# A gated feed-forward kernel: three w1 subtractions moved from a chunk's end to its first steps, and one w2 sum rounded a step sooner

## The chip, the cores and the metric

The kernel runs on one core of a Trainium2 chip. A core has TensorE (matmuls, called PE in the profile; its weight loads are PEld), VectorE (DVE), ScalarE (ACT), GpSimd (POOL) and SyncE (SP), which issues most of the transfers. Each engine works through its own list of instructions in order and waits on semaphores; an instruction that waits holds up all that stand behind it on its engine. The metric is device time in microseconds (us) of one execution, lower is better. A profiled execution leaves a trace in which every instruction has a start and a duration.

## The reference

x has 2048 rows of 576 numbers. The rows are normalised (xn), and two branches work on xn: a linear attention with 32 heads, and a feed-forward network with a hidden width of 4608. The feed-forward part is the one in which the change acts.

```python
xn = _layernorm(x, axis=-1)
s = _A_ref(xn, A_wqkv, A_wo)                      # linear attention, then @ wo
h = _gelu(einsum("bsd,df->bsf", xn, w1) + b1)     # 576 -> 4608
g = _silu(einsum("bsf,fd->bsd", h, w2) + b2)      # 4608 -> 576
return x + s * g
```

## The kernel before

**Products.** Every fp32 operand is split into a high part (a cast to the format that TensorE reads, `set_hi` on ScalarE, L921) and a low part (the rest, `set_lo` on VectorE, L924), and a product is made of three matmuls: high x high, high x low, low x high. Besides, each product of 2 x 2 blocks is made with seven block products in place of eight (a Strassen scheme), so sums and differences of blocks of x, w1, w2 and of the hidden tiles are needed as operands. The products are numbered 1 to 7.

**Stages.** The first 280 us or so are the attention branch. Then the feed-forward network runs over two halves of the 2048 rows, and in each half over nine chunks of 512 hidden columns (`step` counts the 18 chunks; `half, c = divmod(step, 9)`). A chunk has two column pairs for the first product (class `Up`, L1147): each pair needs seven operands from w1. Then come the seven block products with w2 (function `product`, matmuls at L1287, tiles `pm`), in the order 1, 2, 7, 4, 5, 3, 6, each twice (for two groups of rows). VectorE adds each result to `macc` (L1295 or L1297; in chunk 0 L1302 to L1306). Products 2, 3 and 4 go on in the PSUM banks of products 1, 5 and 7: product 3 adds to what product 5 left, and so must wait until VectorE has read product 5's result out of the bank.

**Weights, first half only.** In the first half the chunks also prepare the operands from w1 and w2 for the chunk that follows; they are stored to DRAM too, and the second half only loads them. For w1, a pair n is an object of class `W1`: its raw block (640 KB, tile `w1raw`, L932) is loaded by SyncE into one of two buffers; `T(i)` makes four differences on GpSimd (5 at L946 into the tile `w1t5`, 6 at L948 into `w1t6`, 7 at L951 in place, 4 at L954 in place); `hi(i)` and `lo(i)` round the operands a, 6, 7, 5, b and 4, and `lo` stores each. `w1t5` and `w1t6` exist once each, so a pair's difference 5 waits until the difference 5 of the pair before has been split. The difference 4 overwrites raw data that the operand a reads, and so must follow `lo("a")`. A chunk works on two pairs: in its first steps on its own second pair (table `P1`), and later on the first pair of the next chunk (table `P0`). For w2, `load_sum`, `sum4` and `sum7` build two sums by transfers that accumulate (L497, issued on GpSimd; `sum4(1)` adds the second sum to the first, with which the operand 4 is whole), and `hi` and `lo` round the operands.

**Hidden tiles.** Class `HOps` makes the sums of the hidden tiles on GpSimd: `S(7)` at L1254, `S(5)` at L1245, `S(6)` at L1248, `S(3)` at L1251, for each pair; they wait for the gelu on ScalarE (L1155), and `hi` and `lo` round them (tiles `h_h`, `h_l`).

**What sets the order.** A chunk has 28 steps (`NS`): steps 0 to 6 follow the seven products of the first pair, 7 to 13 those of the second, and 14 to 27 the fourteen of w2. A list `plans` holds what is to be issued behind each step (`add(step, fn)`, `at_step(step)`), in the order of the adds. Order is kept as written on VectorE, ScalarE, GpSimd and TensorE by `in_order`; SyncE's transfers follow the order in which they were issued. So the tables of numbers are the order of the program. `plan_w1` puts a pair's T, hi and lo at the steps of its table, and is itself called at a step, since the pair's object has to exist by then.

Of the kernel before, what the change touches and what calls it, by code (L numbers as in the profile page):

```python
# [42 lines left out]
def linear_attention_gated_ffn(ctx, tc, x, wqkv, wo, w1, b1, w2, b2, out):  # L43
# [97 lines left out]
    class Weight:  # L141
# [28 lines left out]
        def sums(self, raw, eng):  # L170
# [6 lines left out]
            a, b = self.t  # L177
            T = {4: a[:, 0], 5: a[:, 1], 6: b[:, 0], 7: b[:, 1]}
            for i, u, v in ((5, f1a, f0a), (6, f1b, T[5]), (7, f1b, f1a), (4, f0b, T[6])):
                eng.tensor_tensor(T[i], u, v, op=SUB)  # L180

# [339 lines left out]
    def add(step, fn, *args):  # L521
        plans.setdefault(step, []).append((fn, args))

    def at_step(step):
        for fn, args in plans.pop(step, ()):
            fn(*args)
# [191 lines left out]
    for p in range(1, NPAIR):  # L718
        plan_pair(p)
        base = p * NSP  # L720
# [36 lines left out]
    base = NPAIR * NSP  # L757
# [100 lines left out]
    def transpose_p(r, s):  # L858
        pb = p_bufs[s]
        pt = psT.tile([P, 1024], F32, tag="pt", name=f"ptp{r}{s}")  # L860
        for k in range(KT):
            nc.tensor.transpose(pt[:, k * P : (k + 1) * P], pb[:, k * P : (k + 1) * P], ident)
        th = t2.tile([P, KT, P], F32R, tag="th", name=f"th{r}{s}", bufs=3)
        tl = t2.tile([P, KT - 1, P], F32R, tag="tl", name=f"tl{r}{s}", bufs=3)
        pT[r, s] = (th, tl)
        pts[r, s] = pt[:, : KT * P].rearrange("p (k c) -> p k c", k=KT)
# [59 lines left out]
    class W1:  # L926
# [10 lines left out]

        def T(self, i):

            a, b = slice(0, 2), slice(2, 4)  # L940
            f0, f1, src = self.f0, self.f1, self.src
            tt = EW1.tensor_tensor
            if i in (5, 6):
                src[i] = w1p.tile([P, 2, P], F32, tag=f"w1t{i}", name=f"w1t{i}", bufs=1)
            if i == 5:
                tt(src[5], f1[:, a], f0[:, a], op=SUB)  # L946
            elif i == 6:
                tt(src[6], f1[:, b], src[5], op=SUB)  # L948
            elif i == 7:
                src[7] = f1[:, a]  # L950
                tt(src[7], f1[:, b], f1[:, a], op=SUB)  # L951
            else:
                src[4] = f0[:, b]
                tt(src[4], f0[:, b], src[6], op=SUB)  # L954
# [39 lines left out]
    w1t, w2_raw0 = {}, []  # L994
# [5 lines left out]
    for r in range(NPAIR + 2):  # L1000
        base = (NPAIR + r) * NSP
# [35 lines left out]
        if 3 <= r <= 7:  # L1037
            n = 2 * r + 3
# [40 lines left out]
        elif r == NPAIR:  # L1079
# [10 lines left out]
            for j in (5, 6, 7):  # L1090
                w.T(j)
            transpose_p(r - 1, 0)
            p_hi(r - 1, 0), p_lo(r - 1, 0)
            pad(1)
            w.hi("a"), w.lo("a")
            w.T(4)
            at.part(7, 14)
# [90 lines left out]
    class W2:  # L1188
# [34 lines left out]
        def load(self, i):  # L1223
            t, self.ops[i] = op_tile(fr, [2, HD], f"w2_{i}", 1, f"w2_{self.n}_")
            nc.sync.dma_start(t.bitcast(F32), w2_dram[self.n % NC, i])
# [215 lines left out]
    def plan_w1(add, w, base, T, hi, lo):  # L1441
        for table, what in ((T, w.T), (hi, w.hi), (lo, w.lo)):
            for i, at in table.items():
                add(base + at, what, i)

    P1 = dict(
        T={5: 0, 6: 0, 7: 1, 4: 2},
# [1 line left out]
        lo={"a": 0, 6: 1, 7: 2, 5: 3, "b": 4, 4: 4},  # L1449
    )  # L1450
    P0 = dict(
        T={5: 24, 6: 24, 7: 25, 4: 25},
        hi={"a": 24, 6: 25, 7: 26, 5: 26, "b": 27, 4: 27},
        lo={"a": 24, 6: 25, 7: 26, 5: 26, "b": 27, 4: 27},
    )
# [18 lines left out]
    def make(cls, table, n):  # L1474
        table[n] = cls(n)
# [7 lines left out]
    for step in range(n_chunks):  # L1483
        half, c = divmod(step, NC)
        base = step * NS
        plain = step == n_chunks - 1
        h = HOps(c)
        if half == 0:
            plan_w1(add, w1t[2 * step + 1], base, **P1)
            w2c = w2t[step]  # L1490
            if not step:
                w2c.src[7] = w2c.B(0, 1)
                add(base + 2, w2c.sum7)
            for i, at in (PW2 if step else PW2_FIRST).items():
                add(base + at, w2c.hi, i)
                add(base + at, w2c.lo, i)
            if step == 0:
                for i, at in W2_SUMS_FIRST.items():
                    add(at, w2t[0].load, i)
        if half == 0 and c < NC - 1:  # L1500
            add(base + 0, make, W1, w1t, 2 * step + 2)
            add(base + 4, make, W1, w1t, 2 * step + 3)
            add(base + 13, lambda n=2 * step + 2: plan_w1(add, w1t[n], base, **P0))
            make(W2, w2t, step + 1)
            nxt = w2t[step + 1]
            add(base + 0, nxt.load_sum, 4)
            add(base + 12, nxt.sum4, 0)
            add(base + 5, nxt.load_sum, 7)
            add(base + 16, nxt.sum7)
            add(base + (8 if step else 10), nxt.load_raw)  # L1510
            add(base + 21, nxt.hi, 2)
            add(base + 21, nxt.lo, 2)
            add(base + 21, nxt.sum4, 1)
            add(base + 27, nxt.hi, 4)
            add(base + 27, nxt.lo, 4)
            for i, at in W2_SUMS_NEXT.items():
                add(base + at, lambda i=i, n=step + 1: w2t[n].load(i))
        elif not plain:
            add(base + (14 if half == 0 else 7), make, W1Loaded, w1t, 2 * step + 2)
            swap = half == 0  # L1520
            add(base + (22 if swap else 14), make, W1Loaded, w1t, 2 * step + 3)
            if step + 2 < n_chunks:
                make(W2, w2t, step + 1)
                for i, at in W2_NEXT.items():
                    add(base + at + 11 * swap, lambda i=i, n=step + 1: w2t[n].load(i))
            else:
                make(W2, w2t, step + 1)
                add(base + 7, w2t[step + 1].load_raw)
        if not plain:
            if half == 0 and c == NC - 1:  # L1530
                for k, at in ((2, 12), (3, 12), (1, 13), (0, 13)):
                    add(base + at, x_swap, k)
                add(base + 25, silu_first, C11)
                for k in range(2):
                    add(base + 26 + k, combine, C12, nc.vector, slice(2 * k, 2 * k + 2))
                    add(base + 26 + k, combine, C21, nc.gpsimd, slice(2 * k, 2 * k + 2))
            for what in ("S", "hi", "lo"):
                for (i, pr), at in PH[what].items():
                    add(base + at, getattr(h, what), i, pr)
        else:  # L1540
            for f in range(CF):
                w2t[step].plain(f)
                add(base + (1, 2, 3, 8)[f], w2t[step].hi, ("p", f))
                add(base + (2, 3, 8, 9)[f], w2t[step].lo, ("p", f))
        if half == 1 and c == 0:
            add(base, silu_first, C12)
            add(base, silu_first, C21)
            add(base, combine, C22, nc.vector, slice(0, 2))
            add(base + 1, combine, C22, nc.vector, slice(2, 4))
            add(base + 1, silu_first, C22)  # L1550
        if half == 1 and 1 <= c <= 8:
            for k in range(2):
                tiles = {}
                def load(k=k, t=7 + c, tiles=tiles):
                    tiles[0] = finish_tiles(k)
                    finish_load(t, k, tiles[0])
                add(base, load)
                add(base + 4, lambda k=k, t=7 + c, tiles=tiles: finish(t, k, tiles[0]))
        if plain:
            for m in (C12, C21, C22):  # L1560
                add(base + 4, combine, m, nc.gpsimd)
            for t, at in enumerate((5, 5, 7, 13, 5, 12, 12, 12)):
                add(base + at, load_xs, t)
            for b, f, at, lo in (
                (0, 0, 7, 8), (0, 1, 8, 9), (1, 0, 10, 10), (1, 1, 10, 11), (0, 2, 11, 12),
                (0, 3, 12, 13), (1, 3, 13, 13), (1, 2, 13, 13),
            ):
                add(base + at, tail_split, b, f)
                add(base + lo, tail_lo, b, f)
        for j in range(CF // 2):  # L1570
            n = 2 * step + j
            u = Up(n, w1t.pop(n), xs)
            for k, i in enumerate(UP):
                u.step(i)
                h.add(j, u.g)
                at_step(base + 7 * j + k)
        if plain:
            break
        held = {}
        for k, i in enumerate(ORDER):  # L1580
            for q2 in (0, 2):
                product(c, i, q2, [h.ops[i, 0], h.ops[i, 1]], w2t[step].ops[i], held)
                at_step(base + 14 + 2 * k + q2 // 2)
# [36 lines left out]
```

## Time and profile before

| what | value |
|---|---|
| median of 3 runs | 1117.99 us (1117.21 to 1118.75) |
| profiled execution, its own time | 1118.17 us |
| span of its trace (first to last instruction) | 1116.4 us |
| TensorE busy | 98% of the span |
| VectorE, ScalarE, GpSimd busy | 73%, 45%, 42% of the span |
| granted TensorE clock | 1.00 |
| HBM read and written | 165.94 MB and 100.01 MB, 238 GB/s over the span |

The profiled execution lies 0.18 us above the median. Its span is 1.8 us shorter than its time; that is start and end around the instructions, which the trace doesn't show. Timeline rows give start, duration, engine, line, operation, what is written and read by the program's names, the shape, the number of instructions, and in brackets the idle time of the engine before it with what ended it. The list of waits gives total, number and longest. The rows of a source line give the least, median and greatest duration in ns, then the first and last start. Chunks are counted from 0; chunk 2 is the one from about 377 to 423 us.

### The profile page before, as it was taken

The page shows a single profiled execution, that of the slowest core. Times are in us where ns is not written, and L with a number is a line of the kernel's source. Part 1 is how long each engine was busy: PE and PEld are TensorE (multiplying, and loading weights), DVE is VectorE, ACT ScalarE, POOL GpSimd, SP SyncE. Part 2 cuts the span into 40 slices and gives each one's busy share as a digit, 9 for nine tenths or more (in the row PEclk, how much of TensorE's full clock was granted, in tenths as well). Part 3 has the DMA queues.
Part 4 walks back from the last instruction along what each step waited for, and adds up shares of the span by engine and source line. Part 5 has one row for each costly group of instructions (what it writes and reads, how often), then busy time and mean ns, then how long its engine had stood idle before and what let it go on. Part 6 is the DMA issues. An engine that isn't in the chain of part 4 may idle for free.

```text
span 1116.4 us, 18757 instructions
## 1 busy us (share of the span) xinstructions
PE 1095.4 (98%) x6924; PEld 1014.2 (91%) x6924; DVE 812.6 (73%) x1242; ACT 504.2 (45%) x913; POOL 466.1 (42%) x419
## 2 busy tenths in 40 slices
PE   8999999999999999999999999999999999999997
PEld 7899999999898898988989889899898998988987
DVE  6877667877688888888888887666475574664766
ACT  6766555554544444454443544424233243242351
POOL 5854433655354353543535433323224133242340
PEclk9999999999999999999999999999999999999999
DMA  5888747785988879588796869978766666766243
GB/s 203 301 261 280 253 135 224 250 285 188 358 270 308 265 236 355 177 296 272 229 357 185 288 235 382 359 252 282 225 204 213 214 200 216 226 200 218 85 142 114
DMA packets 95531, 271.92 MB, mean 244 GB/s; under 512 B 10381, under 2 KB 21133, under 8 KB 93391
## 3 DMA queue, kind: packets, MB, share of 16 engines
q1 hardware_dynamic: 90543, 260.68, 66.2%
q0 software_dynamic: 4896, 10.03, 5.3%
q8 instruction: 55, 0.90, 0.3%
q14 instruction: 37, 0.30, 0.1%
HBM read 165.94 MB, written 100.01 MB: 238 GB/s over the span
## 4 chain that ended last, share of the span: by engine, by line
PE 88%; DVE 4%; DMA 3%; ACT 2%; issue 1%; POOL 1%; SPq 0%; DVEq 0%; POOLq 0%; ACTq 0%
PE pm L1287 30%; PE e L1147 12%; PE a L1147 10%; PE zy L1147 10%; PE pl L411 5%; PE ps_s L894 5%; PE b L1147 4%; PE e L356 2%; DMA xH<-x_dram 2%; PE a L356 2%; PE z L356 2%; PE pd L1410 2%; PE ps_kva L464 1%; PE b L356 1%; DVE h_l L924 1%
## 5 line engine op out<-in xcount | busy, mean ns | idle before, releaser
L921 ACT CAST h_h<-g 128x512 fp32r<-128x512 f32 x204 | 120.1, 621 | 138.9 <-PE pm L1287 137.8
L924 DVE TENSOR_TENSOR h_l<-g,h_h 128x512 fp32r<-128x512 f32 x204 | 159.5, 782 | 0.0
L1295 DVE TENSOR_TENSOR macc<-macc,pm 128x576 f32<-128x576 f32 x128 | 96.2, 751 | 37.7 <-PE pm L1287 36.0
L1254 POOL TENSOR_TENSOR mid<-g 128x512 f32<-128x512 f32 x34 | 43.9, 1292 | 181.6 <-ACT g L1155 181.6
L1147 PE MATMUL a<-xH,wa 128*128 128x512 f32 x360 | 117.2, 390 | 0.5 <-DMA xH<-x_dram 0.5
L1297 DVE TENSOR_TENSOR macc<-pm,macc 128x576 f32<-128x576 f32 x90 | 68.2, 757 | 25.4 <-PE pm L1287 24.4
L1155 ACT ACTIVATE g<-b,b1c 128x512 f32<-128x512 f32 x36 | 24.8, 688 | 125.0 <-DVE b L1173 125.0
L1147 PEld LDWEIGHTS a<-xH,wa 128*128 128x128 f32 x360 | 67.6, 188 | 14.4 <-DMA xH<-x_dram 0.7
L1147 PE MATMUL e<-xSH,wb 128*128 128x512 f32 x216 | 66.6, 390 | 0.2 <-DVE b L1173 0.2
L1164 ACT COPY mid<-a 128x512 f32<-128x512 f32 x36 | 21.2, 588 | 91.2 <-PE a L1147 91.1
L1248 POOL TENSOR_TENSOR g<-g 128x512 f32<-128x512 f32 x34 | 49.5, 1456 | 22.2 <-DVE h_l L924 20.9
L1381 POOL TENSOR_TENSOR fin1l<-fin1h,fin1l 128x288 f32<-128x288 f32 x8 | 6.4, 805 | 121.9 <-DMA fin1l<-s_dram 63.0
L1147 PE MATMUL a<-xL,wa 128*128 128x512 f32 x144 | 56.2, 390 | 0.0
L1251 POOL TENSOR_TENSOR g<-g 128x512 f32<-128x512 f32 x34 | 49.9, 1467 | 13.1 <-DVE h_l L924 11.8
L1167 DVE TENSOR_TENSOR mid<-b,mid 128x512 f32<-128x512 f32 x36 | 24.6, 685 | 37.5 <-PE b L1147 37.4
L1147 PE MATMUL b<-xSH,w 128*128 128x512 f32 x144 | 50.2, 389 | 0.0
L1147 PE MATMUL zy<-xSH,w 128*128 128x512 f32 x144 | 50.2, 389 | 0.0
L1147 PE MATMUL e<-xSH,w 128*128 128x512 f32 x144 | 50.2, 389 | 0.0
L1147 PE MATMUL zy<-xH,w 128*128 128x512 f32 x144 | 50.2, 389 | 0.0
L1147 PEld LDWEIGHTS e<-xSH,wb 128*128 128x128 f32 x216 | 40.5, 188 | 9.0 <-DVE b L1173 0.6
L1245 POOL TENSOR_TENSOR g<-g 128x512 f32<-128x512 f32 x34 | 47.1, 1386 | 2.7
L1155 ACT ACTIVATE g<-e,b1c 128x512 f32<-128x512 f32 x36 | 24.8, 688 | 49.2 <-DVE e L1180 49.2
(932 smaller groups left out, 3594.2 us busy)
## 6 DMA issues: line engine op xcount, KB each, us to landing
op<-w SPq DMA_DIRECT2D x72, 256.0 KB
w<-op SPq DMA_DIRECT2D x72, 256.0 KB
w1raw<-w SPq DMA_DIRECT2D x18, 640.0 KB
w2raw<-w SPq DMA_DIRECT2D x10, 1152.0 KB
op_a<-wa SPq DMA_DIRECT2D x18, 640.0 KB
wa<-op_a SPq DMA_DIRECT2D x18, 640.0 KB
op<-w2o SPq DMA_DIRECT2D x19, 576.0 KB
w2r<-w SPq DMA_DIRECT2D x6, 1152.0 KB
```

Source lines behind the costliest of these rows:

```text
L356: nc.tensor.matmul(ps, st, mv, start=first and n == 0, stop=n == len(seq) - 1, skip_group_check=True,)
L411: nc.tensor.matmul(self.ps[n], st, self.wk(hl, k, n), start=(i == 0), stop=(i == n_all - 1))
L894: nc.tensor.matmul(self.ps[h], st[:, k, :], w[:, k, h * HD : (h + 1) * HD], start=(i == 0), stop=(i == len(self.seq) - 1),)
L921: nc.scalar.copy(pair[0], src)
L924: eng.tensor_tensor(pair[1], src, pair[0].bitcast(F32), op=SUB)
L1147: nc.tensor.matmul(ps.rearrange("p (c j) -> p c j", c=4), st, mv, start=first and n == 0, stop=n == len(seq) - 1, skip_group_check=True,)
L1155: nc.scalar.activation(g, ps, AF.Gelu_apprx_tanh, bias=b1c[:, f : f + 1])
L1248: tt(src[6, pr], src[5, pr], A(0, 0), op=ADD)
L1251: tt(src[3, pr], src[6, pr], A(0, 1), op=SUB)
L1287: nc.tensor.matmul(ps[:, q, :HD], hs[p][st][:, cs], m[:, p, :], start=(n == 0 and i not in CHAIN), stop=(n == len(seq) - 1), skip_group_ch ...
L1295: nc.vector.tensor_tensor(dst, dst, src, op=SUB)
L1297: nc.vector.tensor_tensor(dst, src, dst, op=ADD)
```

## The change

Two entries move, both in the first eight chunks of the first half. The differences 5, 6 and 7 of the next chunk's first w1 pair are issued at steps 5, 5 and 6 and no longer at 24, 24 and 25; for this `plan_w1` is called at step 4, where the second pair's raw load is issued also. The difference 4 and all roundings of that pair stay at steps 24 to 27. And the operand 4 of the next chunk's w2 is rounded at step 26 and no longer at 27.

```diff
@@ -1449,7 +1449,7 @@
     P0 = dict(
-        T={5: 24, 6: 24, 7: 25, 4: 25},
+        T={5: 5, 6: 5, 7: 6, 4: 25},
         hi={"a": 24, 6: 25, 7: 26, 5: 26, "b": 27, 4: 27},
         lo={"a": 24, 6: 25, 7: 26, 5: 26, "b": 27, 4: 27},
@@ -1500,7 +1500,7 @@
-            add(base + 13, lambda n=2 * step + 2: plan_w1(add, w1t[n], base, **P0))
+            add(base + 4, lambda n=2 * step + 2: plan_w1(add, w1t[n], base, **P0))
@@ -1511,8 +1511,8 @@
-            add(base + 27, nxt.hi, 4)
-            add(base + 27, nxt.lo, 4)
+            add(base + 26, nxt.hi, 4)
+            add(base + 26, nxt.lo, 4)
```

On GpSimd, from the end of chunk 1 to the beginning of chunk 2 (w1raw_4101 is the raw block of pair 4, w1raw_4177 that of pair 5, w1raw_4605 that of pair 6; L1254 is the first sum of the hidden tiles):

```order
-L946 TENSOR_TENSOR w1t_4501<-w1raw_4101 128x256
-L948 TENSOR_TENSOR w1t_4503<-w1raw_4101,w1t_4501 128x256
-L951 TENSOR_TENSOR w1raw_4101<-w1raw_4101 128x256
-L954 TENSOR_TENSOR w1raw_4101<-w1raw_4101,w1t_4503 128x256
+L954 TENSOR_TENSOR w1raw_4101<-w1raw_4101,w1t_4194 128x256
 L946 TENSOR_TENSOR w1t_4596<-w1raw_4177 128x256
 L948 TENSOR_TENSOR w1t_4598<-w1raw_4177,w1t_4596 128x256
 L951 TENSOR_TENSOR w1raw_4177<-w1raw_4177 128x256
 L954 TENSOR_TENSOR w1raw_4177<-w1raw_4177,w1t_4598 128x256
+L946 TENSOR_TENSOR w1t_4696<-w1raw_4605 128x256
+L948 TENSOR_TENSOR w1t_4698<-w1raw_4605,w1t_4696 128x256
+L951 TENSOR_TENSOR w1raw_4605<-w1raw_4605 128x256
 L1254 TENSOR_TENSOR mid<-g 128x512
```

Pair 4's three differences are gone from the end of chunk 1 (they stand at that chunk's beginning now), its difference 4 stays, and pair 6's three stand in chunk 2 behind those of pair 5 and ahead of the hidden tiles' sums.

On VectorE, the last rows of chunk 1 (w_2__4568 before and w_2__4544 after are the w2 operand 4; w_4 and wb are operands of pair 4; the rows of L1295 read the two results of product 6):

```order
-L924 TENSOR_TENSOR w_4_4544<-w1raw_4101,w_4_4544 128x256
-L924 TENSOR_TENSOR w_4_4546<-w1t_4501,w_4_4546 128x256
-L1295 TENSOR_TENSOR macc<-macc,pm_4554 128x2x288
-L924 TENSOR_TENSOR w_2__4568<-w2s_2_4103,w_2__4568 128x576
+L924 TENSOR_TENSOR w_2__4544<-w2s_2_4103,w_2__4544 128x576
+L924 TENSOR_TENSOR w_4_4549<-w1raw_4101,w_4_4549 128x256
+L924 TENSOR_TENSOR w_4_4551<-w1t_4192,w_4_4551 128x256
+L1295 TENSOR_TENSOR macc<-macc,pm_4559 128x2x288
 L924 TENSOR_TENSOR wb_4575<-w1raw_4101,wb_4575 128x384
```

The subtraction of the w2 operand moved from behind the last read of product 6 to ahead of two w1 parts and of that read. ScalarE's casts move in the same way, and on SyncE the store of the w2 operand goes ahead of the stores of operands 7 and 5 of w1 and of one load.

## The prediction

> **What bounds the kernel now.** I read the page first, then the list of waits, then the matmul groups of the second product, then one chunk's end in the timeline, and last the stretch into which work is moved.
>
> ```profile
> PE 1095.4 (98%) x6924; PEld 1014.2 (91%) x6924; DVE 812.6 (73%) x1242; ACT 504.2 (45%) x913; POOL 466.1 (42%) x419
> ...
> PE pm L1287 <- DVE macc L1295: 6.4, 7, 1.1
> ...
> PE pm L1287 <- ACT h_h L921: 0.7, 1, 0.7
> ```
>
> TensorE is busy for 98% of the span, so only what shortens its few waits or lengthens them counts. The two rows of the waits are eight waits of the second product, 7.1 us together: one in each of the eight chunks in which the change acts (0 to 7 of the first half). Next, where the first product of a chunk starts: chunk 0, chunk 8, the first chunk of the second half, and the eighth of that half.
>
> ```profile
> L1287 PE MATMUL pm<-w__3632,h_h x2: 293/294/296, 307.1 to 307.3; 128*128 128x288 f32 x2
> ...
> L1287 PE MATMUL pm<-w__7667,h_h x2: 293/294/296, 676.8 to 676.9; 128*128 128x288 f32 x2
> ...
> L1287 PE MATMUL pm<-w__8054,h_h x2: 293/294/296, 722.7 to 722.8; 128*128 128x288 f32 x2
> ...
> L1287 PE MATMUL pm<-w__10970,h_h x3: 293/293/296, 1038.4 to 1038.8; 128*128 128x288 f32 x3
> ```
>
> Eight chunks of the first half take 676.8 - 307.1 = 369.7 us, 46.21 each. Seven of the second half, with the same matmuls, take 1038.4 - 722.7 = 315.7 us, 45.10 each. So the eight carry 8 x 1.11 = 8.9 us beyond the bare matmul time: 7.1 us as waits, the rest (about 0.2 us a time) in the restart after each wait. The most that this change can win is 8.9 us. Why TensorE waits is seen at the end of chunk 2. Rows of one engine overlap by some 0.07 us, so I go from start to start.
>
> ```profile
> L1287 PE MATMUL pm<-w__4568,h_h x16: 295/295/297, 409.2 to 412.2; 128*128 128x288 f32 x16
> L1287 PE MATMUL pm<-w__4482,h_h x16: 295/295/297, 412.4 to 415.4; 128*128 128x288 f32 x16
> ...
> 412.43 0.89 POOL L497 DMA_DIRECT2D w2s<-w2s  x1 [4.19 <-DMA w2s<-w]
> ...
> 412.99 1.09 POOL L946 TENSOR_TENSOR w1t<-w1raw 128x256 f32<-128x256 f32 x1
> 413.30 1.41 DVE L924 TENSOR_TENSOR w__4944<-w2raw,w__4944 128x576 fp32r<-128x576 f32 x1
> 414.16 1.14 POOL L948 TENSOR_TENSOR w1t<-w1raw,w1t 128x256 f32<-128x256 f32 x1
> 414.63 1.22 DVE L924 TENSOR_TENSOR h_l<-g,h_h 128x512 fp32r<-128x512 f32 x1
> 415.27 1.18 POOL L951 TENSOR_TENSOR w1raw<-w1raw 128x256 f32<-128x256 f32 x1
> ...
> 415.78 0.74 DVE L1295 TENSOR_TENSOR macc<-macc,pm 128x576 f32<-128x576 f32 x1
> ...
> 416.44 0.68 DVE L924 TENSOR_TENSOR h_l<-g,h_h 128x512 fp32r<-128x512 f32 x1
> ...
> 416.67 0.51 PE L1287 MATMUL pm<-w__4707,h_h 128*128 128x288 f32 x2 [0.88 <-DVE macc L1295]
> ```
>
> Product 3 adds to the PSUM bank in which product 5 stands, so it cannot start before VectorE has read product 5's first half (L1295). A product lasts 412.4 - 409.2 = 3.2 us; product 3 is due at 412.43 + 3.2 = 415.63 and starts at 416.67. VectorE is late because two of its subtractions, 413.30 and 414.63, run beside GpSimd's three subtractions for the next w1 pair. Alone they are short:
>
> ```profile
> 387.38 0.76 DVE L924 TENSOR_TENSOR w__4676<-w2s,w__4676 128x576 fp32r<-128x576 f32 x1
> 388.06 0.69 DVE L1180 TENSOR_TENSOR e<-e,mid 128x512 f32<-128x512 f32 x1
> ...
> 398.64 0.68 DVE L924 TENSOR_TENSOR h_l<-g,h_h 128x512 fp32r<-128x512 f32 x1
> ```
>
> So 1.41 - 0.76 = 0.65 and 1.22 - 0.68 = 0.54 us, together 1.19 us, come from that overlap.
>
> **The change, part by part.** *Taken from the chunk's end: L946, L948, L951.* VectorE's path, anew: w2 low part at 413.30, the next row 0.68 us later (387.38 to 388.06), so h_l at 413.98; from 416.44 to product 5's second read in the same spacing as its 0.68 us less the overlap, 0.61 us, so L1295 at 414.59. Its end is 415.33, and the step from its end to the matmul is 416.67 - (415.78 + 0.74) = 0.15 us: TensorE may go on at 415.48, 0.15 us ahead of the 415.63 at which it arrives. The wait goes whole: -1.11 us in each of eight chunks, -8.9 us. What is late next: the sixth matmul of product 3 reads the second h_l (416.44 now); it moves to 415.26 and ends at 415.94, and is needed at 415.63 + 5 x 0.133 = 416.30 (3.2 us for 24 matmuls). That holds. The bound on the other side is no gain, if these two rows stay long.
>
> *Put into steps 5 and 6 of the same chunk.* The three now stand on GpSimd behind the w1 raw load of the same chunk and ahead of the sums of the hidden tiles (L1254 to L1251). Chunk 2 shows the place; the first row is from chunk 0's preparation, where GpSimd did wait for such a load, and the second has that load's issue as its first start.
>
> ```profile
> 276.80 0.73 POOL L946 TENSOR_TENSOR w1t<-w1raw 128x256 f32<-128x256 f32 x1 [2.21 <-DMA w1raw<-w]
> ...
> L932 SPq DMA_DIRECT2D w1raw<-w x18: 332/580/960, 271.7 to 621.6; - x18
> ...
> 382.75 0.33 SPq L932 DMA_DIRECT2D w1raw<-w  x1
> ...
> 390.15 1.29 POOL L1254 TENSOR_TENSOR mid<-g 128x512 f32<-128x512 f32 x1 [8.08 <-ACT g L1155]
> ...
> 394.20 1.29 POOL L1248 TENSOR_TENSOR g<-g 128x512 f32<-128x512 f32 x1 [0.99 <-DVE h_l L924]
> 396.19 1.29 POOL L1251 TENSOR_TENSOR g<-g 128x512 f32<-128x512 f32 x1 [0.70 <-DVE h_l L924]
> ...
> 401.35 1.28 POOL L1254 TENSOR_TENSOR mid<-g 128x512 f32<-128x512 f32 x1 [3.07 <-ACT g L1155]
> ```
>
> GpSimd stands idle for 8.08 us before 390.15. L946 needs the buffer of the pair before, free once that pair's difference is split, and the raw load, issued at 382.75. No wait shows when that load lands. The load of 271.7 took 276.8 - 271.7 = 5.1 us, which would make 387.9. But the queue is full here:
>
> ```profile
> DMA packets 667, 1.87 MB, mean 301 GB/s; under 512 B 74, under 2 KB 74, under 8 KB 666
> ...
> op<-w SPq DMA_DIRECT2D x3, 256.0 KB
> op_a<-wa SPq DMA_DIRECT2D x1, 640.0 KB
> w1raw<-w SPq DMA_DIRECT2D x1, 640.0 KB
> w__4573<-op SPq DMA_DIRECT2D x1, 576.0 KB
> op<-w__4568 SPq DMA_DIRECT2D x1, 576.0 KB
> op_b<-wb SPq DMA_DIRECT2D x1, 384.0 KB
> ...
> 382.75:391.00 8.25, 8.25 (x38) 6.84 (x37) 5.51 (x11) 5.64 (x11) 0.85 (x1) 1.00 1.02 377
> ```
>
> From 376.6 to 382.8 us transfers of 768 + 640 + 640 + 576 + 576 + 384 = 3584 KB (3.67 MB) are issued and 1.87 MB moved; the other 1.8 MB at the 377 GB/s of the last row take 4.8 us, to 387.6, and each 0.9 MB left from before adds 2.4 us: estimate 388 to 391. Three subtractions take 3 x 0.73 = 2.2 us alone, 3.4 us in the overlapped rows. So L1254 starts 0.2 (388 + 2.4) to 4.3 us (391 + 3.4) late. Who waits for that: nothing on GpSimd beyond 401.35, as the idle 0.99 + 0.70 + 3.07 = 4.76 us takes it up. ScalarE and VectorE do have instructions behind L1254's result:
>
> ```profile
> 395.72 0.61 ACT L921 CAST h_h<-mid 128x512 fp32r<-128x512 f32 x1
> ...
> 400.30 0.30 PE L1287 MATMUL pm<-w__4651,h_l 128*128 128x288 f32 x1
> ```
>
> The cast at 395.72 needs L1254's end: at 391 + 3.4 + 1.3 = 395.7 it still starts on time. The sums then overlap VectorE's h_l of 395 to 399 in other places. The last that matters is the one at 398.64 (to 399.32), which the matmul at 400.30 reads: slack 400.30 - 0.15 - 399.32 = 0.83 us. One full set of collisions again costs 1.19 us and would leave 0.36 us of wait a chunk; none leaves nothing. I take 0.1 us, nearer to nothing because the landing is late only in part of the chunks: 8 x 0.1 = +0.8 us; ends 0 and +2.9.
>
> The Trainium skill ("SBUF — State Buffer", Who interferes with whom) says that a VectorE operation with two SBUF inputs and a GpSimd operation that reads SBUF exclude each other for the whole instruction, and that the first to start wins. The trace agrees at 413.30: that row ends 0.63 us after L946's end at 414.08, as if it had been held and then run. By this rule the collisions move with the three subtractions and do not vanish; the sum would be that of the second rival below.
>
> *Third w2 sum a step sooner (L924 on w2s, step 26 for 27).* On ScalarE its cast now follows the w1 cast of step 25, on VectorE its subtraction stands ahead of two w1 parts. The cast of step 25, and the time from issue to landing of the transfer that ends the sum:
>
> ```profile
> 416.85 0.40 ACT L921 CAST w<-w1t 128x256 fp32r<-128x256 f32 x1
> ...
> w2s<-w2s POOLq DMA_DIRECT2D x1, 288.0 KB, 3.5
> ```
>
> The sum lands at 412.43 + 3.5 = 415.9, 1.3 us ahead of the cast's turn at 416.85 + 0.40 = 417.25. VectorE's last read of product 6 moves back by one subtraction of 0.76 us less the idle time before it; the bank has two other banks ahead of it in rotation. The store goes ahead of two smaller ones and one load on SyncE's queue, whose next readers are a chunk away. Cost 0, bounds -0.1 and +0.3 us a chunk (a late P1 set by half a subtraction).
>
> *Sum:* -8.9 + 0.8 + 0 = -8.1 us. The profiled execution took 1118.17 us, 0.18 above the median of the runs, 1117.99: forecast 1118.17 - 8.1 = 1110.1 there, 1109.9 as a median.
>
> **Rivals.** 1. *Half of it stays.* The margin of 0.15 us is thin: if VectorE is 0.5 us late by another overlap (the DMA issue at 412.43 beside 413.30), a wait of 0.35 us and the 0.2 of the restart stay, half of the 1.11; 8 x 0.56 = 4.5 us are won: 1113.5 us. For it: the thin margin. Against: the row at 398.64 shows the lone length.
> 2. *The collisions move to product 1* (the other side). Three subtractions each hold VectorE for up to 0.73 us, 2.2 us on its path to 399.32; less the slack 0.83 that makes 1.4 us in eight chunks, +11 - 8.9 = +2.3 us: 1120.3. It decides once VectorE reaches the h_l of 398.64 more than 0.83 + 1.11 = 1.94 us late. Against: VectorE is busy for only 5.51 of the 8.25 us in the row 382.75:391.00 (its third pair of numbers counts it), so part of a delay is made up.
> 3. *GpSimd held by the load.* If the load lands at 394, L1254 ends 394 + 3.4 + 1.3 = 398.7, 3 us behind the cast at 395.72; less 0.8 slack, 2.2 us a chunk: +17.6 - 8.9 = +8.7, 1126.7. Turning point, a delay of 1.94 us again: landing at 395.72 + 1.94 - 4.7 = 393.0. Against: the estimate 388 to 391.
> 4. *Nothing*: the overlap is not what stretches the two rows, VectorE is late anyway: 1118. Against: the second halves of both durations agree with lone rows of the same shape.
>
> **The numbers.** Full gain 0.64 (1108.8 to 1111.5, the likeliest, 1109.9); half 0.16; nothing 0.06; collisions moved 0.07; held by the load 0.07. The first two hold 0.8, so the range is 1108.8 to 1115.7: below, the whole 8.9 us (1109.1) and 0.1 us in some chunks from the third sum; above, where a gain can just be told. 0.2% (2.2 us) is what can be told from no change. Faster 0.80; same 0.07, the fourth rival and the mild end of the second; slower 0.13, the rest.
>
> **What would show it.** Right: no wait of L1287 for L1295; the w2 low part in step 21 at 0.76 and its follower at 0.68 us; chunks of 45.1 to 45.3 us; L946 waiting for w1raw until 388 to 391, L1254 late by 0.2 to 4.3 us, and at 401.35 on time. Wrong: a new wait at the first product's matmuls for h_l or h_h, or the idle time before the second L1254 used up.

## The result and the profile after

The changed kernel takes 1108.94 us (median of six runs, 1108.34 to 1111.02); the kernel before, in six runs, 1117.82 us. The ratio is 0.992, 95% interval 0.9909 to 0.993: 8.9 us faster. The forecast was 1109.9 us in a range of 1108.8 to 1115.7; the median lies in it, 1.0 us below the forecast and only 0.1 us above the range's lower end; two of the six runs (1108.34 and 1108.43 us) lie below that end.

The page's first rows of the changed kernel, and the last row of the answer that lists what TensorE waited for (twelve rows in all; none of them is L1287):

```profile
span 1107.5 us, 18744 instructions
...
PE 1094.3 (99%) x6924; PEld 1014.3 (92%) x6924; DVE 803.6 (73%) x1242; ACT 504.1 (46%) x913; POOL 461.4 (42%) x419
...
PE e L1147 <- DVE b L1173: 0.2, 1, 0.2
```

TensorE is busy for nearly as long as before (1094.3 against 1095.4 us); the span is shorter by 8.9 us (1107.5 against 1116.4), and the eight waits of the second product are gone. Where the first product starts in chunk 0 and in chunk 8:

```profile
L1287 PE MATMUL pm<-w__3632,h_h x2: 293/294/296, 307.7 to 307.8; 128*128 128x288 f32 x2
...
L1287 PE MATMUL pm<-w__7667,h_h x2: 293/294/296, 668.5 to 668.6; 128*128 128x288 f32 x2
```

Eight chunks take 668.5 - 307.7 = 360.8 us, 45.10 each: as long as a chunk of the second half, so no wait is left to win in them. That is 369.7 - 360.8 = 8.9 us. The end of chunk 2 in the timeline, and the groups of products 5 and 3:

```profile
410.47 0.89 POOL L497 DMA_DIRECT2D w2s<-w2s  x1 [4.03 <-DMA w2s<-w]
...
411.51 0.75 DVE L924 TENSOR_TENSOR w__4949<-w2raw,w__4949 128x576 fp32r<-128x576 f32 x1
412.18 0.68 DVE L924 TENSOR_TENSOR h_l<-g,h_h 128x512 fp32r<-128x512 f32 x1
412.78 0.75 DVE L1295 TENSOR_TENSOR macc<-macc,pm 128x576 f32<-128x576 f32 x1
413.44 0.69 DVE L924 TENSOR_TENSOR h_l<-g,h_h 128x512 fp32r<-128x512 f32 x1
...
L1287 PE MATMUL pm<-w__4487,h_h x16: 295/296/297, 410.6 to 413.6; 128*128 128x288 f32 x16
L1287 PE MATMUL pm<-w__4711,h_h x16: 295/295/298, 413.8 to 416.8; 128*128 128x288 f32 x16
```

The two subtractions that took 1.41 and 1.22 us take 0.75 and 0.68 us. VectorE reads product 5's bank from 412.78 to 413.53, and product 3 starts 3.2 us behind product 5, without a gap. And the stretch into which the three subtractions went, GpSimd's rows first, then one of ScalarE and three of VectorE:

```profile
389.11 1.00 POOL L946 TENSOR_TENSOR w1t<-w1raw 128x256 f32<-128x256 f32 x1 [9.00 <-DMA w1raw<-w]
390.19 0.74 POOL L948 TENSOR_TENSOR w1t<-w1raw,w1t 128x256 f32<-128x256 f32 x1
390.89 0.75 POOL L951 TENSOR_TENSOR w1raw<-w1raw 128x256 f32<-128x256 f32 x1
391.59 1.74 POOL L1254 TENSOR_TENSOR mid<-g 128x512 f32<-128x512 f32 x1
393.40 1.66 POOL L1245 TENSOR_TENSOR g<-g 128x512 f32<-128x512 f32 x1
395.14 1.62 POOL L1248 TENSOR_TENSOR g<-g 128x512 f32<-128x512 f32 x1
396.84 1.85 POOL L1251 TENSOR_TENSOR g<-g 128x512 f32<-128x512 f32 x1
...
399.56 1.28 POOL L1254 TENSOR_TENSOR mid<-g 128x512 f32<-128x512 f32 x1
...
387.47 0.69 ACT L1155 ACTIVATE g<-zy,b1c 128x512 f32<-128x512 f32 x1
...
391.41 0.77 DVE L924 TENSOR_TENSOR h_l<-g,h_h 128x512 fp32r<-128x512 f32 x1
...
394.57 1.04 DVE L924 TENSOR_TENSOR h_l<-mid,h_h 128x512 fp32r<-128x512 f32 x1 [0.67 <-ACT h_h L921]
...
396.85 0.68 DVE L924 TENSOR_TENSOR h_l<-g,h_h 128x512 fp32r<-128x512 f32 x1
```

GpSimd waits 9.0 us for the raw load and then works without a pause up to the second L1254. The first L1254 could have started at 387.47 + 0.69 = 388.2 and starts 3.4 us later; TensorE does not wait for it. In the kernel before, the sums of the hidden tiles stood alone on GpSimd in this stretch, and VectorE's rows beside them were long already:

```profile
390.66 1.40 DVE L924 TENSOR_TENSOR w__4707<-w2raw,w__4707 128x576 fp32r<-128x576 f32 x1 [1.32 <-ACT w__4707 L921]
...
395.01 1.03 DVE L924 TENSOR_TENSOR h_l<-g,h_h 128x512 fp32r<-128x512 f32 x1
...
396.37 1.66 DVE L924 TENSOR_TENSOR h_l<-mid,h_h 128x512 fp32r<-128x512 f32 x1 [0.33 <-ACT h_h L921]
```

Over the lone 0.76 and 0.68 us these three carry 0.64 + 0.35 + 0.98 = 1.97 us. In the changed kernel VectorE's rows of the stretch carry 0.09 + 0.36 = 0.45 us (0.77 and 1.04 over 0.68).

### The profile page after: what moved, and what is told of

Its sections match the earlier page's. It is cut to its first block, busy times and chain, and to the rows that moved or that the text cites. A ratio compares the mean times of both kernels' runs of the same rounds, so it can differ in the third digit from the quotient of the medians.

```text
span 1107.5 us, 18744 instructions
## 1 busy us (share of the span) xinstructions
PE 1094.3 (99%) x6924; PEld 1014.3 (92%) x6924; DVE 803.6 (73%) x1242; ACT 504.1 (46%) x913; POOL 461.4 (42%) x419
## 4 chain that ended last, share of the span: by engine, by line
PE 92%; ACT 3%; DVE 2%; issue 1%; POOL 1%; DMA 1%; DVEq 0%; POOLq 0%; ACTq 0%
PE pm L1287 34%; PE e L1147 11%; PE zy L1147 10%; PE a L1147 10%; PE pl L411 5%; PE ps_s L894 5%; PE b L1147 4%; PE e L356 2%; PE a L356 2%; PE z L356 2%; PE pd L1410 2%; PE ps_kva L464 1%; PE b L356 1%; PE ptp L862 1%; PE pt L277 1%
## 5 line engine op out<-in xcount | busy, mean ns | idle before, releaser
L924 DVE TENSOR_TENSOR h_l<-g,h_h 128x512 fp32r<-128x512 f32 x204 | 162.2, 795 | 0.0
L1295 DVE TENSOR_TENSOR macc<-macc,pm 128x576 f32<-128x576 f32 x128 | 96.3, 752 | 36.8 <-PE pm L1287 36.0
L1254 POOL TENSOR_TENSOR mid<-g 128x512 f32<-128x512 f32 x34 | 45.9, 1349 | 102.5 <-ACT g L1155 102.4
L1248 POOL TENSOR_TENSOR g<-g 128x512 f32<-128x512 f32 x34 | 50.9, 1498 | 17.8 <-DVE h_l L924 16.1
L1251 POOL TENSOR_TENSOR g<-g 128x512 f32<-128x512 f32 x34 | 52.4, 1542 | 10.7 <-DVE h_l L924 7.6
L946 POOL TENSOR_TENSOR w1t<-w1raw 128x256 f32<-128x256 f32 x18 | 13.6, 756 | 88.0 <-DMA w1raw<-w 56.1
L1180 DVE TENSOR_TENSOR e<-e,mid 128x512 f32<-128x512 f32 x36 | 25.1, 697 | 30.5 <-PE e L1147 30.4
```

The lines of the kernel that those rows point to most:

```text
L924: eng.tensor_tensor(pair[1], src, pair[0].bitcast(F32), op=SUB)
L1248: tt(src[6, pr], src[5, pr], A(0, 0), op=ADD)
L1251: tt(src[3, pr], src[6, pr], A(0, 1), op=SUB)
L1254: tt(src[7, pr], A(0, 0), A(1, 0), op=SUB)
L1295: nc.vector.tensor_tensor(dst, dst, src, op=SUB)
```

## The experiments

Theory A: three GpSimd subtractions that run beside two VectorE subtractions at the chunk's end hold these up by 1.2 us, and VectorE has only 0.15 us of slack there ahead of the read for which product 3 waits. Rivals: the w2 operand's earlier rounding is what helps (B); the overlap is dear wherever it stands, so the new place has a price too; GpSimd, held by the load, hands a delay on to TensorE.

The runs were made in three groups, each on one chip with runs of the kernel before; on these chips the kernel before took 1116.5, 1116.4 and 1116.7 us (medians). So ratios are compared, and the time of the eight chunks, from one profile of each kernel (first matmul of the first product in chunk 0 to that in chunk 8), which all but ignores the rest of the program:

| run | ratio to before, 95% interval | eight chunks, us |
|---|---|---|
| before / changed kernel | 1 / 0.992 (0.9909 to 0.993) | 369.7 / 360.8 |
| three subtractions moved alone | 0.9928 (0.9911 to 0.9944) | 360.8 |
| w2 operand moved alone | 1.0 (0.9991 to 1.0009) | 368.8 |
| one subtraction back | 0.996 (0.9945 to 0.9975) | 364.7 |
| two subtractions back | 1.0009 (1.0 to 1.0018) | 369.2 |
| the three left out | 0.9935 (0.9918 to 0.9953) | 360.8 |
| raw load at step 4 | 1.0309 (1.0288 to 1.0329) | 403.2 |
| raw load at step 3 | 1.0053 (1.0033 to 1.0073) | 373.6 |
| the three at steps 17 and 18 | 0.9928 (0.9908 to 0.9948) | 360.8 |
| the three at step 12 | 0.9936 (0.9916 to 0.9956) | 361.4 |
| before, VectorE's w2 subtraction moved | 0.9939 (0.9923 to 0.9956) | 362.5 |

**The two parts of the change, one at a time.**

```diff
 # three subtractions moved alone: the changed kernel with
-            add(base + 26, nxt.hi, 4)
-            add(base + 26, nxt.lo, 4)
+            add(base + 27, nxt.hi, 4)
+            add(base + 27, nxt.lo, 4)
 # w2 operand moved alone: the kernel before with the reverse
```

> The three subtractions moved alone, the w2 operand still rounded at step 27. Theory A (the subtractions' overlap with VectorE is the whole cause): 1108.9 +- 0.8 us, first-half chunks of 45.1 us, no wait of L1287 for L1295. Theory B (the earlier rounding of the w2 operand is what shortens VectorE's list, or is needed for the gain): above 1111 us, waits left in the eight chunks.

> The w2 operand rounded at step 26 alone, the three subtractions still at steps 24 and 25. Theory A: 1117.8 +- 0.8 us, the eight waits as before (7.1 us). Theory B: below 1115 us.

The subtractions alone give 1108.76 us and chunks of 45.10 us, the whole gain. The w2 operand alone changes no time that can be told (1116.31 against 1116.51 us); its waits are 4.5 us for L1295 and 1.7 us for h_h, 6.2 in all against 7.1. Theory B falls: that edit is neither needed nor of use.

**One and two of the three put back at the chunk's end.**

```diff
 # the changed kernel with, for one back and for two back
-        T={5: 5, 6: 5, 7: 6, 4: 25},
+        T={5: 5, 6: 5, 7: 24, 4: 25},
+        T={5: 5, 6: 24, 7: 24, 4: 25},
```

> The changed kernel with one of the three subtractions (7, L951) back at step 24. It runs at about 411.0 us of chunk 2's time in the changed kernel, 0.5 us ahead of VectorE's w2 subtraction at 411.5. Theory A, with the later one held until the earlier ends: VectorE 0.26 us later against a margin of 0.15 us, so a wait of about 0.1 us, with the restart 0.1 to 0.3 us in each of eight chunks: 1109.9 to 1111.5 us. If the cost went by the number of subtractions: a third of 8.9 us, 1111.9 us.

> The changed kernel with two of the three (6 and 7) back at steps 24. Theory A: the second holds VectorE's h_l too, VectorE about 1.0 us later against the margin of 0.15: 0.7 to 1.0 us a chunk, 1114.5 to 1117 us. By their number: two thirds of 8.9 us, 1114.9 us; the waits of L1287 for L1295 back, 0.6 to 0.9 us each.

One back costs 364.7 - 360.8 = 3.9 us, two cost 8.4, all three (the kernel before) 8.9. One is above both forecasts, which allowed 0.8 to 2.4 us or a third of 8.9; with two, the profile's 8.4 us are 1.05 us a chunk, just above "0.7 to 1.0 us a chunk", and the time, 1117.57 us, is 0.6 us above its range (and 0.1% above the kernel before on the same chip: nothing of the gain is left). The end of chunk 2 with one back:

```profile
412.15 0.89 POOL L497 DMA_DIRECT2D w2s<-w2s  x1 [4.16 <-DMA w2s<-w]
412.36 0.76 DVE L1297 TENSOR_TENSOR macc<-pm,macc 128x576 f32<-128x576 f32 x1 [0.24 <-PE pm L1287]
412.71 1.10 POOL L951 TENSOR_TENSOR w1raw<-w1raw 128x256 f32<-128x256 f32 x1
413.04 1.39 DVE L924 TENSOR_TENSOR w__4948<-w2raw,w__4948 128x576 fp32r<-128x576 f32 x1
414.36 0.68 DVE L924 TENSOR_TENSOR h_l<-g,h_h 128x512 fp32r<-128x512 f32 x1
...
415.84 0.50 PE L1287 MATMUL pm<-w__4711,h_h 128*128 128x288 f32 x2 [0.32 <-DVE macc L1295]
```

and with two:

```profile
412.78 1.10 POOL L948 TENSOR_TENSOR w1t<-w1raw,w1t 128x256 f32<-128x256 f32 x1
413.41 1.78 DVE L924 TENSOR_TENSOR w__4946<-w2raw,w__4946 128x576 fp32r<-128x576 f32 x1
413.50 1.07 POOL L951 TENSOR_TENSOR w1raw<-w1raw 128x256 f32<-128x256 f32 x1
415.11 0.68 DVE L924 TENSOR_TENSOR h_l<-g,h_h 128x512 fp32r<-128x512 f32 x1
...
416.61 0.50 PE L1287 MATMUL pm<-w__4709,h_h 128*128 128x288 f32 x2 [0.71 <-DVE macc L1295]
```

In both, VectorE's w2 subtraction ends 0.62 us after the last GpSimd row (412.71 + 1.10 = 413.81 and 414.43; 413.50 + 1.07 = 414.57 and 415.19): it is held to the end and then runs. My forecast for one was wrong on the length of the hold: I took the subtraction as 0.74 us from 411.03 on, 0.26 us beside VectorE's. Its row lasts 1.10 us, VectorE is held by 1.39 - 0.76 = 0.63 us, and less 0.15 of slack that makes 0.48; a chunk loses 0.49 us on average (3.9 / 8). With two the hold is 1.78 - 0.76 = 1.02 us, less the slack 0.87, and a chunk loses 1.05 on average. Chunk 2 alone loses 0.55 us with one back and 0.93 with two, and 1.11 in the kernel before, whose hold is 1.19. The other chunks agree: the holds differ from chunk to chunk, from 0.32 us (one back, chunk 5) to 1.66 (two back, chunk 0), and in all eight chunks of these two runs, of the kernel before and of the run with the w2 operand alone, the loss is the chunk's own hold less 0.08 to 0.09 us. That is the slack of 0.15 less some 0.07 us by which a matmul starts late behind each wait (417.01 - 416.67 = 0.34 us for two starts in the kernel before, 2 x 0.133 elsewhere). So the loss goes by the hold less the slack, not by the number of subtractions.

**What the new place costs.** The three left out altogether (these operands are then cut from the raw block):

```diff
-        T={5: 5, 6: 5, 7: 6, 4: 25},
+        T={4: 25},
...
+            self.src |= {5: self.f0[:, :2], 6: self.f1[:, :2], 7: self.f1[:, 2:4]}
...
```

> The changed kernel without the three subtractions of the first pair of each next chunk (operands 5, 6 and 7 of that pair are then cut from the raw block, so w1's differences are left out of the computation there). Theory A, with a second place that costs nothing: as the changed kernel, 1108.9 +- 0.5 us. If the second place costs the 0.1 us a chunk that was forecast: 1108.1 us; if it costs 0.36: 1106.

The run gives 1108.88 us and the same 360.8 us of the eight chunks. The new place costs nothing that can be told; the forecast's 0.8 us for it is not there.

**Two other places for the three.**

```diff
 # the changed kernel with
-        T={5: 5, 6: 5, 7: 6, 4: 25},
+        T={5: 17, 6: 17, 7: 18, 4: 25},
+        T={5: 12, 6: 12, 7: 12, 4: 25},
```

> The three subtractions at steps 17 and 18, between the two accumulating transfers on GpSimd: they run at about 406.1 to 408.5 us of chunk 2's time, beside VectorE's h_l at 406.8 and 408.3. Theory A (an overlap costs only where VectorE's slack is smaller than the hold): each hold is 0.3 to 0.7 us, the slack of the bank reads there is about 0.45 us: 0 to 0.3 us a chunk, 1108.9 to 1111.5 us. If an overlap with h_l costs TensorE wherever it stands: 1115 us or more.

> The three subtractions at step 12, behind the first accumulating transfer and ahead of the second pair's sums, in GpSimd's idle 3 us there: 396.2 to 398.6 us of chunk 2's time, beside the h_l of 396.85 that the matmul at about 398.5 reads with 0.8 us of slack. Theory A: one hold of up to 0.7 us fits the slack: 1108.9 to 1110 us. The second rival of the forecast (collisions moved to product 1): 0.3 us or more a chunk, 1111.5 us or more.

At steps 17 and 18, in chunk 2:

```profile
405.58 1.03 POOL L946 TENSOR_TENSOR w1t<-w1raw 128x256 f32<-128x256 f32 x1
406.16 1.02 DVE L924 TENSOR_TENSOR h_l<-g,h_h 128x512 fp32r<-128x512 f32 x1
406.69 1.08 POOL L948 TENSOR_TENSOR w1t<-w1raw,w1t 128x256 f32<-128x256 f32 x1
407.09 0.74 DVE L1295 TENSOR_TENSOR macc<-macc,pm 128x576 f32<-128x576 f32 x1
407.73 0.74 POOL L951 TENSOR_TENSOR w1raw<-w1raw 128x256 f32<-128x256 f32 x1
407.76 1.26 DVE L924 TENSOR_TENSOR h_l<-g,h_h 128x512 fp32r<-128x512 f32 x1
```

VectorE is held twice, 0.34 and 0.58 us over the lone 0.68, 0.92 us against 1.19 in the kernel before, and TensorE loses nothing: 360.8 us, ratio 0.9928. At step 12 seven chunks are at 45.10 us; chunk 0 loses 0.6 us (a wait of 0.4 us for a cast of the hidden tiles). So an overlap that holds VectorE does not have to cost TensorE anything.

**The overlap left in place, the slack made larger.** VectorE's w2 subtraction is taken out from ahead of the bank read, in the kernel before:

```diff
-            add(base + 21, nxt.hi, 2)
-            add(base + 21, nxt.lo, 2)
+            add(base + 26, nxt.hi, 2)
+            add(base + 26, nxt.lo, 2)
```

> The kernel before, with the three subtractions at steps 24 and 25 as they were, and VectorE's w2 subtraction of step 21 (operand 2, 0.76 us alone) moved to step 26. If the wait is a matter of the slack ahead of product 5's bank read (0.15 us with that subtraction in place, 0.8 us without it), the three may go on overlapping: VectorE is 0.5 to 0.7 us late, no or hardly a wait, 7.5 to 8.9 us faster than before. If running beside GpSimd is bad in itself there: 3 us faster at the most.

```profile
411.85 1.09 POOL L946 TENSOR_TENSOR w1t<-w1raw 128x256 f32<-128x256 f32 x1
412.06 1.43 DVE L924 TENSOR_TENSOR h_l<-g,h_h 128x512 fp32r<-128x512 f32 x1
413.01 1.08 POOL L948 TENSOR_TENSOR w1t<-w1raw,w1t 128x256 f32<-128x256 f32 x1
413.42 0.74 DVE L1295 TENSOR_TENSOR macc<-macc,pm 128x576 f32<-128x576 f32 x1
414.06 0.73 POOL L951 TENSOR_TENSOR w1raw<-w1raw 128x256 f32<-128x256 f32 x1
414.08 1.26 DVE L924 TENSOR_TENSOR h_l<-g,h_h 128x512 fp32r<-128x512 f32 x1
...
415.40 0.40 PE L1287 MATMUL pm<-w__4707,h_l 128*128 128x288 f32 x1 [0.18 <-DVE h_l L924]
```

VectorE is held by 0.75 and 0.58 us, more than in the kernel before, and yet 7.2 us of the eight chunks are won (369.7 to 362.5); by the ratio 6.8 us, a little under the forecast's 7.5 to 8.9. The bank read is on time; what is late next is the second h_l, for which product 3's later matmul waits 0.2 us in this chunk. So the wait needs both: the hold, and a VectorE list without slack behind it. The 1.7 us that remain (362.5 - 360.8) are lost in six of the chunks, 0.14 to 0.48 us each; the other two lose nothing.

**GpSimd held by the load.**

```diff
 # the changed kernel with
-            add(base + 0, make, W1, w1t, 2 * step + 2)
+            add(base + 4, make, W1, w1t, 2 * step + 2)
 # and with base + 3
```

> The changed kernel with the raw load of that pair issued at step 4 and not at step 0, behind the stores of steps 1 to 4 on SyncE's queue: issue at about 389.5 us of chunk 2's time, landing at about 394.5, which is 1.5 us past the turning point 393.0 of the forecast. If GpSimd held by the load reaches TensorE: L1254 about 7 to 8 us late, its cast on ScalarE 4.6 us late, less 0.8 us of slack, 3 to 6 us in each of eight chunks, 1130 to 1155 us. If GpSimd makes up for it: 1109 us.

> The changed kernel with that raw load at step 3, behind the store of a w2 operand: issued 4 to 5 us later than in the changed kernel, landing 2 to 4 us later (388.7 in chunk 2 there, so 391 to 393). With 0.8 us of slack at product 1's h_l, and the cast of L1254's result due at 393.9 there, a landing past about 390 reaches TensorE: 0.5 to 3 us in each chunk, 4 to 25 us slower than the changed kernel. If GpSimd's idle time takes it up: as the changed kernel.

Both are slower, as forecast. With the load at step 3, chunk 2:

```profile
395.07 0.74 POOL L946 TENSOR_TENSOR w1t<-w1raw 128x256 f32<-128x256 f32 x1 [12.65 <-DMA w1raw<-w]
...
397.61 1.28 POOL L1254 TENSOR_TENSOR mid<-g 128x512 f32<-128x512 f32 x1
...
398.92 0.62 ACT L921 CAST h_h<-mid 128x512 fp32r<-128x512 f32 x1 [2.57 <-POOL mid L1254]
...
399.58 1.23 DVE L924 TENSOR_TENSOR h_l<-mid,h_h 128x512 fp32r<-128x512 f32 x1 [3.22 <-ACT h_h L921]
...
401.33 1.16 DVE L924 TENSOR_TENSOR h_l<-g,h_h 128x512 fp32r<-128x512 f32 x1
...
402.54 0.40 PE L1287 MATMUL pm<-w__4649,h_l 128*128 128x288 f32 x1 [1.18 <-DVE h_l L924]
```

This is the chain of the third rival row by row: load, L946, L1254, the cast, VectorE's list, product 1. The delay costs (373.6 - 360.8) / 8 = 1.6 us a chunk; in this chunk, L946 starts at 395.07. With the load at step 4, where L946 starts at 406.63 in a chunk 2 that itself begins later, a chunk loses 5.3 us. Not all of that is waiting: in six stretches of the eight chunks, some 27 us together, the profile shows a granted TensorE clock of 0.50, as here in chunk 2 (the stretch and its length, busy time and instructions of PE, PEld, DVE, ACT and POOL, the clock, the busy share of the DMA engines, GB/s):

```profile
411.90:418.60 6.70, 5.72 (x22) 5.38 (x23) 4.21 (x6) 2.85 (x6) 6.46 (x6) 0.50 0.33 62
```

In these stretches 105 matmuls start 0.24 us apart and not 0.133, which makes some 11 of the 42.4 us that the eight chunks lose; about 3.9 us a chunk remain for the waits. With the load at step 3 the clock is 1.00 in all eight chunks.

## Why the prediction was right

- *The bound.* 8.9 us were the most to be won, from chunks of 46.21 and 45.10 us; the eight chunks gave 8.9. The mechanism is shown from both sides: put back in parts, the subtractions bring the wait back by hold less slack; with the slack made larger, an overlap of that size costs 1.7 us in the eight chunks in place of 8.9. That the span falls by the same 8.9 us is partly luck: outside the eight chunks, chunk 8 is 0.6 us shorter, and chunk 0 starts 0.5 us later.
- *VectorE's new path.* The bank read was forecast 414.59 - 412.43 = 2.16 us behind product 5's start, the second h_l 2.83 us; they stand at 412.78 - 410.6 and 413.44 - 410.6, 2.2 and 2.8 us. The margin of 0.15 us held in all eight chunks, so the first rival (half stays) did not come about.
- *The new place: the term that was mis-sized.* It was put at +0.8 us (ends 0 and 2.9) and measured 0: 360.8 us with the three and without. The step that failed is "one full set of collisions again". The rows show why it was too dear: the prediction let VectorE be the one that is held, here and in its second rival (1120.3 us), and in chunk 2 it is GpSimd that is: the first and last of its four sums take 1.74 and 1.85 us where they took 1.29, while VectorE's h_l at 396.85 takes its lone 0.68 us beside the last. GpSimd had idle time for that. Nor was the stretch free of holds before: VectorE's rows there lose 0.45 us where they lost 1.97. The measured median is 1.0 us under the forecast; 0.8 of it is this term.
- *The load.* L946 was forecast between 388 and 391, L1254 0.2 to 4.3 us late, the second L1254 on time; L946 started at 389.11 and L1254 at 391.59, with product 1 of this chunk 1.8 us earlier than before. In the times of the kernel before that is 390.9 and 393.4: at the late end of the forecast, and L1254 3.2 us late. And the second L1254 stands 1.7 us behind product 1's start, as before (399.56 - 397.85, and 401.35 - 399.64). The slack taken as the third rival's limit is real: past it a chunk loses 1.6 us with the load at step 3, and 5.3 at step 4, of which some 1.4 are the lower clock. The rival's price was about right too: it put a landing at 394 at 2.2 us a chunk; at step 3, L946 of chunk 2 starts at 394.5 in the times of the kernel before (product 1 at 400.17 against 399.64), and that chunk loses 2.2 us.
- *The third w2 sum.* Forecast 0; the run with it alone and the run without it agree.
- *Not settled.* The kernel before waits 0.5 us for a reload of x in chunk 8, the changed one does not. It is not the eight chunks' doing alone: with two subtractions back, or with the w2 operand moved alone, it is gone too, at the old speed. Its cause stays open.

## What to carry to other kernels

Ask of each instruction ahead of a PSUM read how much slack there is before the matmul that waits for it, and move the other engine's work away only where that slack is smaller than the hold: the same overlap cost 1.1 us a chunk ahead of product 5's read and nothing 5 us earlier. When work is moved ahead of others on an in-order queue, look for its latest input: here a load that was ready in time at step 0 cost 1.6 us a chunk when issued at step 3 and 5.3 at step 4, where the lower clock came on top. A step number is no time: GpSimd ran the subtractions of steps 24 and 25 from the beginning of product 5 (step 22) on, as soon as the wait for the accumulating transfer ahead of them had ended.

## What the runs showed of the hardware

- VectorE's two-input subtraction is held until GpSimd's has ended, not slowed in proportion: with one and two back it ends 0.62 us after the last GpSimd row, in the kernel before 0.63 us after L946. The Trainium skill ("SBUF — State Buffer", Who interferes with whom) has the exclusion and that the first to start wins.
- A waiting VectorE can be passed over by a second GpSimd subtraction, but need not be. With two back it is held through L948 and L951 (1.78 us). In the kernel before it gets in between L946 and L948, and again between L948 and L951: h_l at 414.63 ends at 415.85, 0.55 us behind L948, and L951 then takes 1.18 us. A dependence of the second subtraction on the first does not decide it: L951 uses nothing that L948 writes, and the same pair lets VectorE in once and once not. What decides it is not shown.
- A GpSimd row that follows a transfer issued there begins before the issue has ended (412.71 against 412.15 + 0.89 = 413.04) and is longer by about that overlap: 1.10 us in the run with one subtraction back, where rows that meet nothing last 0.73 to 0.75. The lone duration, counted from the start of the row, therefore gave too short a hold in the forecast for that run.
